# Twelve units instead of sixteen turned by TensorE, and part of VectorE's early work on GpSimd

## The chip, the cores and the metric

The kernel runs on one core of a Trainium2 chip. The metric is the device time of one execution in microseconds. PE is TensorE, DVE is VectorE, ACT is ScalarE, POOL is GpSimd and SP is SyncE, whose queue issues most of the loads.

## What is computed

A recurrent attention block (RWKV5) feeds a dense block with the activation h - tanh(h). Everything is float32, apart from the two weight matrices, which arrive as float64 and are converted on the chip.

```python
# r, k, v: (4, 8, 768, 48); w, u: (8, 48); w_in: (384, 2048); w_out: (2048, 384)
for t in range(S):
    kt, vt, rt = (k[:, :, t], v[:, :, t], r[:, :, t])
    cur = np.einsum('bhd,bhe->bhde', u[None] * kt, vt)
    y[:, :, t] = np.einsum('bhd,bhde->bhe', rt, state + cur)
    state = w[None, :, :, None] * state + np.einsum('bhd,bhe->bhde', kt, vt)
...
x = np.ascontiguousarray(attn_out.transpose(0, 2, 1, 3)).reshape(B * S, H * D)   # (3072, 384)
h = x @ w_in
g = h - np.tanh(h)
return (g @ w_out).astype(np.float32)
```

## The kernel before

**Attention in 24 units.** A unit (function `unit`, L754) is 64 time steps of two batches (one per half of the 128 partitions), all eight heads. `kw` is k times falling powers of the decay (L951). r and k must be turned so that the head dimension lies on the partitions. In the first way, used by units 0 to 15, PE turns r and kw with four transposes each (`turn`, L793 to L795) into the PSUM tile `x_ps`; DVE scales r by the table `w_up` (L799) and ACT copies k (L832). In the second way, used by units 16 to 23, r and k are loaded a second time: SP spreads them with eight small DMAs each into places inside `parts` (`spread_out`, L806 to L814), DVE turns 32x32 squares (L818) and multiplies by the powers of the decay or their reciprocals (L819). PSUM then holds only `yk_ps`.

After that a unit goes on alike: PE multiplies the state by rT (`from_state`) and kT by rT (`levels`), DVE copies the lower triangle of the levels into `at` (L981), PE multiplies `at` by v and kw by v (`outputs`, `to_state`; all of these matmuls carry the line L750), ACT copies the result to `xt` and `rest` (L910), and DVE adds to the state (L937) and lets it decay (L990). The diagonal of `at` is r times k (L836) times u (L971), summed (L840), written by ACT (L844). In the second way the state products come first and an ACT copy of two numbers (L872) stands between them and the levels. Unit n works on the state of unit n - 2.

**Dense part in 12 blocks of two units.** Block j has 256 tokens; its `xt` is completed by six POOL DMAs from `rest` (L931). A tile (function `hidden`, L1030) is two of the 16 slices of the inner dimension: PE computes h (L169), ACT five functions of it (L178 to L186), DVE four operations that end in g (L193 to L199), and PE multiplies g by w_out. There are two ways for that last product. The plain one is four products of 384 columns (L207). The other makes seven products of 192 columns (L258) from sums of g, which POOL makes (L243 to L247), and from sums of w_out, `mixed`, which DVE makes once (L267: four groups of four operations); it needs four PSUM banks that the first way of the units uses as `x_ps`.

**Passes.** For blocks 0 to 5, a first and a second pass over four slices each and a third over eight (`PASSES = 4, 4, 8`); sums between passes lie in `parts`. The third pass uses the seven products, so it starts after the last unit of the first way, after the weights' conversion (L137 to L143: five DVE and two ACT operations for each of 16 pieces) and after the mixing of its slices. Blocks 6 to 11 follow, each in one pass but the last. The places for the second way's loads lie in the part of `parts` that belongs to blocks 0 to 2, and come free in the third pass, when `gather` (L290) has read them.

**The order of all instructions** is found at build time by a planner (class `Plan`, L302). Each task has an engine, a cost, tasks that it follows, and a due time. `forward` simulates the engines, each taking the ready task that is due first; `backward` works out latest times; `search` changes due times at random and keeps what does not lengthen the simulated end. `order` (L479) first searches 2500 times up to 240 us (`BUSY`), then 500 times over the whole. Before the change all units are planned in the first way; then the registered changes turn units 16 to 23 to the second way (`change`, L326), and 500 more tries move only what starts after 240 us. The resulting list is emitted as it is, each engine in its order; waits come from the real data dependencies. `fills` (L683) puts idle matmuls into PE's gaps at the start.

Of the kernel before, what the change touches and what calls it, by code (L numbers as in the profile page):

```python
# [11 lines left out]
F32 = mybir.dt.float32  # L12
# [18 lines left out]
SHORT = 64  # L31
# [10 lines left out]
SEVEN = 8  # L42

# [102 lines left out]
class Dense:  # L146
# [114 lines left out]
    def mix(self, f, x):  # L261

        n, w, pairs = self.d.DM // 2, self.w_out_sb.rearrange("p (f z) n -> p f z n", z=2)[:, f], self.seven.mixed[:, f]
        b11, b12, b21, b22 = w[:, :, 0, :n], w[:, :, 0, n:], w[:, :, 1, :n], w[:, :, 1, n:]
        out, a, b, op = [(0, b11, b12, ALU.subtract), (1, b22, pairs[:, :, 0], ALU.add), (2, b22, b12, ALU.subtract),
                         (3, pairs[:, :, 1], b21, ALU.subtract)][x]
        self.nc.vector.tensor_tensor(pairs[:, :, out], a, b, op)  # L267
# [34 lines left out]
class Plan:  # L302
# [12 lines left out]
    def __init__(self):  # L315
        self.tasks, self.fills, self.changes = [], [], []

    def add(self, engine, cost, run, after=(), due=1e9, data=0, gated=False, steps=0):
        t = SimpleNamespace(engine=engine, cost=cost, run=run, after=[x for x in after if x], due=due, data=data,
                            gated=gated, steps=steps, then=[], n=len(self.tasks))  # L320
        for x in t.after:
            x.then.append(t)
        self.tasks.append(t)
        return t

    def change(self, t, **new):  # L326

        self.changes.append((t, new))
# [149 lines left out]

    def order(self, first=2500, tries=500):  # L479
# [18 lines left out]
        self.search(due, tries, chance, 0.0)  # L498

        for t, new in self.changes:  # L500
            for x in t.after:
                x.then.remove(t)
            vars(t).update(new)
            t.after = [x for x in t.after if x]
            for x in t.after:
                x.then.append(t)
        for _ in range(4):
            plan = self.forward(self.due)
            latest = self.backward(plan)
            self.due = [old if start < self.BUSY else new for old, new, start in zip(self.due, latest, plan[1])]  # L510
        plan = self.search(self.due, tries, chance, self.BUSY)
# [28 lines left out]
def near(ctx, tc, r, k, v, w, u, out, shared, moe_w_in, moe_w_out):  # L540
# [20 lines left out]
    plan = Plan()  # L561
    add = plan.add
# [6 lines left out]

    spread = parts.rearrange("q a n -> q (a n)")  # L570
    blocks = [spread[:, i * 512 : (i + 1) * 512].rearrange("q (x b e) -> q x b e", x=2 * NP, b=SHORT // 32) for i in range(4)]
    again = spread[:, 2048 : 2048 + NP * (SHORT + 1)].rearrange("d (p n) -> d p n", p=NP)
# [83 lines left out]
    inverse = work.tile([128, NP, SHORT + 1], F32, name="inverse", tag="tg")  # L656
    w_up = fixed("w_up", [128, NP, 2, SHORT])
# [25 lines left out]
    def fills(to):  # L683
        def run(n):
# [6 lines left out]
    now = [add(e, 1.25 if e == "ACT" else .87, lambda e=e, at=at, x=x: e_of[e].dma_start(out=rows[at : at + NP, :, :D], in_=x.rearrange("(p i) d -> p i d", i=2)), due=-1, data=.05)  # L691
           for e, at, x in (("SP", 0, w), ("ACT", NP, u))]
    cols = add("PE", .25, lambda: T.transpose(cols_ps, rows.rearrange("p i d -> p (i d)"), ident[: 2 * NP, : 2 * NP]), now)


    now = add("DVE", .45, lambda: V.tensor_scalar(
        by[:, :, 1:], wcol[:, :, None].to_broadcast([128, NP, SHORT]), W_LOW, W_HIGH, ALU.max, ALU.min), [cols])
    now = add("DVE", .7, lambda: V.tensor_tensor_scan(
        power.rearrange(flat), by.rearrange(flat), plus.rearrange(flat), 0.0, ALU.mult, ALU.add), [now])

    ups = add("ACT", .6, lambda: A.copy(w_up, power[:, :, None, :SHORT].to_broadcast([128, NP, 2, SHORT])), [now])
    now = add("DVE", 1.75, lambda: V.reciprocal(inverse, power), [now])
    inverted = now
    doubled = add("ACT", .6, lambda: A.copy(twice, inverse[:, :, None, 1:].to_broadcast([128, NP, 2, SHORT])), [now])
    now = tabled = add("PE", .7, table, [doubled], steps=8)
    downs = add("ACT", .5, lambda: A.copy(w_down, tab.rearrange("s (h d) -> s h d", h=H)[:, :, :D]), [now])
    keeps = add("ACT", .2, lambda: A.copy(saved, cols_ps), [cols])
    w_us = add("POOL", .2, lambda: G.tensor_tensor(w_u, saved[:, :NP], saved[:, NP:], ALU.mult), [keeps])
    now = add("POOL", 1.0, bounds, [keeps])
    now = add("PE", .2, lambda: T.matmul(tab[0:1, 0:1], ok[:, 0, :1], shared["one"], start=True, stop=True), [now, downs])  # L710
    flagged = add("DVE", .15, lambda: V.tensor_scalar(shared["flag"], tab[0:1, 0:1], 128 * NP - 0.5, None, ALU.is_lt), [now])
    bonus = add("SP", .65, lambda: Q.dma_start(
        out=ub.rearrange("p h d -> p (h d)"),
        in_=bass.AP(tensor=u.tensor, offset=u.offset, ap=[[0, 128], [1, H * D]])), data=.7)

    add("ACT", 1.3, lambda: A.activation(fixed("warm", [128, 1]), shared["one"], AF.Tanh), due=0)


    def steps(generator):

        made = []

        def step():
            if not made:
                made.append(generator())
            next(made[0])

        return step

    loads, converted = [], []  # L730
    for n in range(weights.count):

        queues, data = (("SP",), (3.0,)) if n % 4 > 1 else (("SP", "POOL") * 2, (1.2, .95) * 2)
        of = [add(e, .55, lambda n=n, i=i, e=e: weights.load(n, i, e_of[e]), [converted[n - 4] if n >= 4 else None],
                  data=x, gated=True) for i, (e, x) in enumerate(zip(queues, data))]
        if weights.sources[n % 4 > 1].dtype != I64:
            converted.append(of[-1])
            continue
        step = steps(lambda n=n: weights.convert(n))
        now = of + ([converted[n - 2]] if n >= 2 else [])  # L740
        for name, cost in (("DVE", .47), ("DVE", .47), ("ACT", .84), ("ACT", .84), ("DVE", .87), ("DVE", .87), ("DVE", .87)):
            now = [add(name, cost, step, now)]
        converted += now


    def flat4(t):
        return t.rearrange("d p z t -> d (p z t)")

    def put(*args, **how):
        T.matmul(*args, skip_group_check=True, **how)  # L750

    units, filled, last_h = [], {}, {}

    def unit(n):  # L754
# [3 lines left out]
        ch, half = divmod(n, 2)  # L758
        j, slot = divmod(n, L)
        steps_at = slice(ch * SHORT, (ch + 1) * SHORT)  # L760
        t = SimpleNamespace(at=ats[n % 2])
        rt, vt, kw, state = rts[n % (AHEAD + 1)], vts[n % (AHEAD + 1)], kws[n % 2], states[half]
        two = n >= L * (FIRST + 2)
        pair = yk_ps if two else x_banks[n == 1]
        sign = -1.0 if slot and j in dense.negative else 1.0
        r_ps, k_ps = (pair[:, i] for i in range(2))
        lev, own_lev = (pair[:, :, at : at + 256].rearrange("s i (p t) -> s i p t", p=NP) for at in ((256, 0) if two else (0, 256)))
        none = SimpleNamespace(**{x: None for x in "r k v turn rT kw kT rk du own diag state lev cp out xt rest add decay".split()})
        b1, b2, b3 = (units[n - i] if n >= i else none for i in (1, 2, 3))
        x = SimpleNamespace(rest=None, rk=None, du=None, own=None)  # L770
        units.append(x)
        product = n < OWN
        swap = n >= SWAP


        direct = j == 0

        def fetch(name, src, after):
            def run(z):
                if name == "k" and not hasattr(t, "kt"):  # L780
                    t.kt = first_k[slot] if direct else load.tile([128, H, D], F32, name="kt", tag="kt")
                to = {"r": rt, "v": vt}.get(name)
                Q.dma_start(out=(t.kt if to is None else to)[HALF[z], :, :D],  # L783
                            in_=src[half * 2 + z, :, steps_at, :].rearrange("h t d -> t h d"))

            of = [add("SP", .65, lambda z=z: run(z), after, data=.71) for z in range(2)]
            return add("none", 0, lambda: None, of)

        x.r = fetch("r", r, [b3.turn, b3.rk, b1.r])
        x.k = fetch("k", k, [b3.kw, b3.rk, b1.k])  # L790
        x.v = fetch("v", v, [b3.out, b1.v])

        def turn(src, to):  # L793
            for p in range(NP):
                T.transpose(to[:, p * C : (p + 1) * C], src[:, 2 * p : 2 * p + 2, :].rearrange("t h d -> t (h d)"), ident)  # L795
# [26 lines left out]
        def across_r():  # L822
            t.rT = across("rT", 0, power[:, :, :SHORT])
# [601 lines left out]
```

## Time and profile before

| | us |
|---|---|
| median of 3 runs (lowest, highest) | 591.65 (591.44, 592.0) |
| the profiled execution | 591.61 |
| its span | 589.5 |
| busy in it: PE, DVE, ACT, POOL | 571.2, 484.1, 398.9, 208.3 |
| last of the weights' conversion ends (L143) | 203.6 |
| mixing on DVE (L267), first start to last end | 208.4 to 236.4 |
| first of the seven products (L258) | 226.4 |
| first load of the second way (L813) | 268.3 |

The span runs from the first to the last instruction; the execution's time has some 2 us around it. Engines work side by side, so busy times don't add up to the span. A row of a group gives line, engine, operation, output and inputs with their shapes, count, then busy time and mean duration in ns, then the idle time ahead of it and what ended it. Durations of neighbours on PE and DVE overlap slightly; the distance between two starts is what one of them costs its engine.

### The profile page before, as it was taken

The numbers are of one execution on the slowest core, as the hardware profiler recorded it, in microseconds if no ns is written. First come the engines' busy times: TensorE is split into PE (matmuls) and PEld (weight loads), VectorE is DVE, ScalarE is ACT, GpSimd is POOL, SyncE is SP. The second block draws the span as 40 slices with busy tenths as digits, with TensorE's granted clock in tenths as the row PEclk, the third lists the DMA queues.
The fourth block names the chain that finished last, engine by engine and source line by source line (L and its number), as shares of the span: only waits on it lengthen the run. The fifth ranks groups of instructions, "written<-read, shape, count | busy, mean of one in ns | idle before, by whom it ended". The sixth has DMA issues, their size and how long they took to land.

```text
span 589.5 us, 14312 instructions
## 1 busy us (share of the span) xinstructions
PE 571.2 (97%) x5525; PEld 485.0 (82%) x5525; DVE 484.1 (82%) x806; ACT 398.9 (68%) x894; POOL 208.3 (35%) x366
## 2 busy tenths in 40 slices
PE   8888999999999989999999999999999999999996
PEld 5566677777777768999999998989999888999995
DVE  5699969999999999988779889697775896555666
ACT  3698888989686975775555566565665785476652
POOL 6002212201000143555554544483344554363420
PEclk9999999999999999999999999999999999999999
DMA  6976995954411310203111412244121220100101
GB/s 118 201 155 129 161 204 107 126 132 86 93 54 28 62 30 21 39 16 61 36 26 24 85 28 30 40 83 69 35 30 19 38 40 1 25 11 2 28 1 31
DMA packets 121141, 36.91 MB, mean 63 GB/s; under 512 B 113352, under 2 KB 115496, under 8 KB 121064
## 3 DMA queue, kind: packets, MB, share of 16 engines
q1 hardware_dynamic: 115900, 28.73, 26.9%
q0 software_dynamic: 4992, 6.99, 5.4%
q8 instruction: 45, 0.74, 0.5%
q14 instruction: 32, 0.26, 0.1%
q10 hardware_dynamic: 172, 0.20, 0.1%
HBM read 30.08 MB, written 4.72 MB: 59 GB/s over the span
## 4 chain that ended last, share of the span: by engine, by line
PE 76%; DVE 11%; ACT 4%; issue 3%; DMA 3%; SPq 2%; POOL 0%; DVEq 0%; ACTq 0%; POOLq 0%
PE h L169 37%; PE p L258 27%; PE o L207 5%; PE yk_ps L750 5%; SPq L783 2%; DMA st<-in_moe_w_in_dram 2%; DVE tg L197 1%; DVE g L193 1%; DVE tg L195 1%; DVE g L199 1%; DVE rT L799 1%; ACT at L844 1%; ACT s L178 1%; PE x_ps L795 1%; DMA kt<-in_k_dram 1%
## 5 line engine op out<-in xcount | busy, mean ns | idle before, releaser
L169 PE MATMUL h<-xt,w_in_sb 128*128 128x256 f32 x1152 | 281.0, 381 | 1.1 <-DVE w_in_sb L143 0.9
L169 PEld LDWEIGHTS h<-xt,w_in_sb 128*128 128x128 f32 x1152 | 212.9, 190 | 31.4 <-PE x_ps L795 1.1
L243 POOL TENSOR_TENSOR sg<-g 128x256 f32<-128x256 f32 x69 | 53.8, 780 | 144.6 <-DVE g L199 72.5
L258 PE MATMUL p<-mixed,sg 128*128 128x192 f32 x426 | 104.0, 326 | 0.0
L193 DVE TENSOR_TENSOR g<-h,th 128x512 f32<-128x512 f32 x96 | 65.8, 685 | 33.2 <-ACT s L178 14.3
L182 ACT ACTIVATE tg<-h 128x512 f32<-128x512 f32 x96 | 57.2, 596 | 48.3 <-PE h L169 48.2
L195 DVE SCALAR_TENSOR_TENSOR tg<-s,tg 128x512 f32<-128x512 f32 x96 | 68.3, 712 | 25.9 <-ACT tg L182 13.8
L180 ACT ACTIVATE th<-h 128x512 f32<-128x512 f32 x96 | 57.4, 598 | 43.0 <-PE h L169 42.8
L931 POOL DMA_DIRECT2D xt<-rest x66 | 32.3, 496 | 146.0 <-ACT rest L910 146.0
L178 ACT ACTIVATE s<-h 128x512 f32<-128x512 f32 x96 | 57.4, 598 | 39.1 <-PE h L169 38.8
L199 DVE COPY_PREDICATED g<-small,tg 128x512 f32<-128x512 int32 x96 | 76.0, 793 | 4.0
L258 PEld LDWEIGHTS p<-mixed,sg 128*128 128x128 f32 x426 | 75.1, 190 | 0.0
L197 DVE SCALAR_TENSOR_TENSOR tg<-q,tg 128x512 f32<-128x512 f32 x96 | 68.5, 715 | 7.5 <-ACT q L184 4.1
L207 PE MATMUL o<-w_out_sb,g 128*128 128x384 f32 x192 | 69.8, 490 | 1.7 <-DVE g L199 1.6
L258 PE MATMUL p<-w_out_sb,g 128*128 128x192 f32 x284 | 71.1, 332 | 0.0
L184 ACT ACTIVATE q<-s,m1b 128x512 f32<-128x512 f32 x96 | 69.5, 724 | 0.8
L186 ACT ACTIVATE small<-s,smallb 128x512 f32<-128x512 f32 x96 | 69.3, 722 | 0.5
L258 PEld LDWEIGHTS p<-w_out_sb,g 128*128 128x128 f32 x284 | 52.5, 190 | 7.4
L844 ACT ACTIVATE at<-same,du 128x64 f32<-128x64 f32 x184 | 47.7, 343 | 5.7 <-DVE du L840 5.6
L207 PEld LDWEIGHTS o<-w_out_sb,g 128*128 128x128 f32 x192 | 35.5, 190 | 18.4 <-issue 1.9
L245 POOL TENSOR_TENSOR sg<-sg,g 128x128 f32<-128x128 f32 x69 | 44.6, 647 | 5.1
L247 POOL TENSOR_TENSOR sg<-sg,g 128x128 f32<-128x128 f32 x69 | 39.0, 566 | 5.1
(131 smaller groups left out, 684.4 us busy)
## 6 DMA issues: line engine op xcount, KB each, us to landing
st<-in_moe_w_out_dram SPq DMA_DIRECT2D x8, 768.0 KB, 5.4
rt<-in_r_dram SPq DMA_DIRECT2D x48, 96.0 KB, 3.3
vt<-in_v_dram SPq DMA_DIRECT2D x48, 96.0 KB, 2.9
st<-in_moe_w_in_dram SPq DMA_DIRECT2D x16, 288.0 KB, 5.1
kt<-in_k_dram SPq DMA_DIRECT2D x44, 96.0 KB, 3.3
out_dram<-o POOLq DMA_DIRECT2D x44, 96.0 KB, 2.3
st<-in_moe_w_in_dram POOLq DMA_DIRECT2D x16, 96.0 KB, 5.1
xt<-rest POOLq DMA_DIRECT2D x66, 16.0 KB, 2.3
```

Source lines behind the costliest of these rows:

```text
L169: self.nc.tensor.matmul(t.h2[:, z], self.w_in_sb[:, t.f // 2, kk, z * 128 : (z + 1) * 128], self.xts[t.j][:, kk].rearrange("p b t -> p (b ...
L178: A.activation(out, t.h, AF.Square)
L180: A.activation(out, t.h, AF.Tanh)
L182: A.activation(out, t.h, AF.Tanh, scale=G1)
L184: A.activation(out, t.s, AF.Square, bias=self.m1b)
L186: A.activation(out, t.s, AF.Relu, bias=self.smallb, scale=-1.0)
L193: V.tensor_tensor(t.g, t.h, t.th, ALU.subtract)
L195: V.scalar_tensor_tensor(t.tg, t.s, C4, t.tg, ALU.mult, ALU.mult)
L197: V.scalar_tensor_tensor(t.tg, t.q, K1, t.tg, ALU.add, ALU.mult)
L199: V.copy_predicated(t.g, t.small.bitcast(I32), t.tg)
L207: self.nc.tensor.matmul(self.outs[i], t.g2[:, z, i * C : (i + 1) * C], self.w_out_sb[:, t.f + z, :], start=t.first and z == 0, stop=t.last ...
L258: self.nc.tensor.matmul(ps[bank][:, half * n : (half + 1) * n], a, b, start=t.first and half == 0, stop=t.last, skip_group_check=True)
```

## The change

1. Units 0 to 11 (before: 0 to 15) take the first way, 12 to 23 the second. The third pass now follows unit 11, and the second way's first loads follow the gathers of blocks 0 to 2.
2. The mixing of w_out (16 operations) moves from DVE to POOL.
3. For units 8 to 11, four operations each move from DVE to POOL: kw, r times k, that times u, and the decay of the state.
4. The planner builds two plans. A simpler one has sixteen units in the first way and all others turned by PE, as the plan of before had ahead of its registered changes. The real one takes the simpler one's due times for tasks that start there before 90 us (`ALIKE`), and finds the others by five rounds of `forward` and `backward` and 500 tries (`follow`). Registered changes are gone. The planner's cost for a second-way turn is 1.4 instead of 1.22.
5. `inverse` gets a place of its own, so the second reciprocal (L827) goes; the table `w_up` goes, and r is scaled by the powers themselves, read twice through a broadcast.

The body of `near` from the first task on becomes a function `lay_out(early, across_by)`. Without the change of indentation, the core of the diff is:

```diff
+ALIKE = 90.0
+EASED = 8
...
-        self.nc.vector.tensor_tensor(pairs[:, :, out], a, b, op)
+        self.nc.gpsimd.tensor_tensor(pairs[:, :, out], a, b, op)
...
+    def follow(self, other, until, tries=500):
+        theirs = {t.key: (other.due[t.n], t.start) for t in other.tasks}
+        kept = [theirs[t.key][0] if theirs.get(t.key, (0, until))[1] < until else None for t in self.tasks]
+        def pinned(due):
+            return [y if y is not None else x for x, y in zip(due, kept)]
...
+        for _ in range(5):
+            plan = self.forward(pinned(due))
+            due = self.backward(plan)
+        return self.listed(self.search(pinned(due), tries, Random(5), until))
...
-    inverse = work.tile([128, NP, SHORT + 1], F32, name="inverse", tag="tg")
-    w_up = fixed("w_up", [128, NP, 2, SHORT])
+    inverse = fixed("inverse", [128, NP, SHORT + 1])
...
-        two = n >= L * (FIRST + 2)
+        two = n >= early
+        turned = two and across_by == "DVE"
...
+        eased = across_by == "DVE" and EASED <= n < early
+        V_or_G, own_at = (G, ("POOL", 1.0)) if eased else (V, ("DVE", .47))
...
-            V.tensor_tensor(flat4(t.rT), r_ps, flat4(w_up), ALU.mult)
+            V.tensor_tensor(t.rT, r_ps.rearrange("d (p z t) -> d p z t", p=NP, z=2),
+                            power[:, :, None, :SHORT].to_broadcast([128, NP, 2, SHORT]), ALU.mult)
...
-            if n == L * (FIRST + 2):
-                V.reciprocal(again, power)
-            t.kT = across("kT", 1, again[:, :, 1:])
+            t.kT = across("kT", 1, inverse[:, :, 1:])
...
+        if turned:
+            freed = sum((gathered[y] for y in range(3)), []) if n < early + 2 else []
+            in_r = add("SP", 4.8, lambda: spread_out(r, 0), [b2.rT, *freed], data=.8)
+            in_k = add("SP", 4.8, lambda: spread_out(k, 1), [b2.kT, *freed], data=.8)
+        x.turn = None if turned else add("PE", .46, lambda: turn(rt, r_ps), [x.r] + free, steps=8)
+        x.kw = add(*own_at, lambda: V_or_G.tensor_tensor(kw[:, :, :D], t.kt[:, :, :D], w_down, ALU.mult), [x.k, downs, b2.out])
+        x.turn_k = x.rk = None if turned else add("PE", .46, lambda: turn(t.kt if direct else kw, k_ps), [x.k if direct else x.kw] + free, steps=8)
...
+        x.rT = add("DVE", 1.4, across_r, [in_r, b1.lev]) if turned else add("DVE", .62, scale_r, both + [ups])
+        if turned:
+            x.kT = add("DVE", 1.4, across_k, [in_k, b1.lev])
...
+            x.rk = add(*own_at, own, [x.r, x.k, b2.du, b1.rk if not b1.own else None])
+            now = add(*own_at, lambda: V_or_G.tensor_tensor(t.rk, t.rk, ub, ALU.mult), [x.rk, bonus])
...
+        x.decay = x.add if not ch else add(*own_at, lambda: V_or_G.tensor_tensor(state[:, :, :, :D], state[:, :, :, :D], w_all, ALU.mult), [x.add]) if more else None
...
+                now = add(*(("POOL", 1.05) if across_by == "DVE" else ("DVE", .47)), run, converted + [now])
...
-            done = units[L * (FIRST + 2) - 1]
+            done = units[early - 1]
...
-    for t in plan.order():
+    simpler = lay_out(L * (FIRST + 2), "PE")
+    simpler.order()
+    plan = lay_out(L * FIRST, "DVE")
+    for t in plan.follow(simpler, ALIKE):
```

## The prediction

> **What bounds the kernel now.** I read the page's busy rows first, then stretches of the span, because a mean over a start, a middle and a tail says little.
>
> ```profile
> span 589.5 us, 14312 instructions
> PE 571.2 (97%) x5525; PEld 485.0 (82%) x5525; DVE 484.1 (82%) x806; ACT 398.9 (68%) x894; POOL 208.3 (35%) x366
> ...
> 0.00:90.00 90.00, 79.28 (x1452) 56.16 (x1453) 73.00 (x135) 66.48 (x193) 20.38 (x59) 1.00 0.86 161
> 90.00:225.00 135.00, 132.08 (x1255) 99.50 (x1255) 132.10 (x215) 109.48 (x230) 19.26 (x35) 1.00 0.38 77
> 225.00:285.00 60.00, 59.96 (x378) 55.55 (x378) 52.35 (x90) 39.84 (x85) 31.23 (x48) 1.00 0.20 36
> 285.00:510.00 225.00, 224.99 (x2023) 205.35 (x2022) 177.74 (x286) 138.13 (x306) 109.77 (x174) 1.00 0.21 38
> ```
>
> The columns are the stretch, its length, then busy time of PE, PEld, DVE, ACT and POOL, the clock and the DMA share. From 90 us on PE is the bound: it idles 2.9 of 135 us in the second stretch and nothing in the next two. DVE is as full as PE from 90 to 225 (132.1 of 135), and has 47 us free from 285 to 510. POOL is nearly unused before 225. So time is won in two ways: fewer PE instructions, or an end to those 2.9 us. PE's waits in 120 to 225 name who ends them, both DVE operations of units 14 and 15:
>
> ```profile
> PE x_ps L795 <- DVE at L981: 1.4, 1, 1.4
> PE yk_ps L750 <- DVE state L937: 0.6, 1, 0.6
> ```
>
> **PE's part of the change.** Four units (12 to 15) lose two groups of four transposes each. I price a group by the distance between starts in PE's order of time, not by its busy time, since matmuls overlap.
>
> ```profile
> 200.60 0.60 PE L795 MATMUL x_ps<-ident,kw 128*128 128x128 f32 x4
> 201.03 1.46 PE L169 MATMUL h<-xt,w_in_sb 128*128 128x256 f32 x6
> ...
> 205.35 1.46 PE L169 MATMUL h<-xt,w_in_sb 128*128 128x256 f32 x6
> 206.74 0.69 PE L750 MATMUL yk_ps<-rT,state 48*64 48x64 f32 x32
> 207.26 0.65 PE L750 MATMUL x_ps<-rT,kT 48*64 48x64 f32 x32
> 207.84 1.56 PE L169 MATMUL h<-xt,w_in_sb 128*128 128x256 f32 x6
> ...
> 353.82 0.49 PE L258 MATMUL p<-w_out_sb,sg 128*128 128x192 f32 x2
> 354.24 0.69 PE L750 MATMUL yk_ps<-rT,kT 48*64 48x64 f32 x32
> 354.86 0.59 PE L258 MATMUL p<-w_out_sb,g 128*128 128x192 f32 x2
> ```
>
> A group takes 201.03 - 200.60 = 0.43 us (0.49 elsewhere), so two take 0.9. But the second way splits state products from level products (an ACT copy stands between). Joined, as at 206.74, they take 1.10 plus 0.10 at each edge (half an h takes 1.29 undisturbed, 1.39 here): 1.30. Split, the second piece, at 354.24, takes 0.62 plus 0.10 on each side, 0.82, and the first, at 348.55 in the same view, 0.83: 1.65. Net per unit 0.9 - 0.35 = 0.55; four units give **2.2 us**. All of it is on the path, as PE is the path.
>
> **The stretch 90 to 225.** DVE loses there the work of units 12 to 15. By the groups' means a unit is kw 0.588, rk 0.576, times ub 0.597, du 0.543, rT 0.684, cp 0.726, state 0.547 and decay 0.561: 4.8 us, four are 19. Sixteen operations of units 8 to 11 (four of each of kw, rk, times ub, decay) go to POOL: 4 x 2.32 = 9.3. The sixteen of mixing cost DVE 5.9 + 2.7 + 2.2 = 10.8. That is 39 us less, against 132 used (part of the 9.3 lies before 90 us). With DVE at some three quarters, the 2.9 us should mostly go. Bounds: all stay (0) or all go (2.9). I take **1.9**, the two waits above plus rounding down, as both belong to units that leave.
>
> **POOL's new work.** No row shows a 128x384 tensor-tensor on POOL. The nearest rows are its sums of g; uncontended ones take 0.46 us at 128 elements and 0.73 at 256, slowest ones 0.97 and 1.17. A line through the fast pair gives 0.99 at 384, an estimate; below it stands 0.73 (the smaller shape), above it 1.4 (1.17 plus one such step). 32 x 0.99 = 32 us (23 to 45), in a stretch with POOL busy 19 of 135. It is cover enough, provided the queue behind (POOL's loads of w_in, fills of xt) is not late: a fill waits behind at most one chain of a unit, some 3 us, and xt is filled well ahead.
>
> What POOL costs DVE is seen on DVE's own rows: the masked copy without POOL beside it, and with it.
>
> ```profile
> L199 DVE COPY_PREDICATED g<-small,tg 128x512 f32<-128x512 int32 x19 | 13.9, 730 | 0.1
> ...
> L199 DVE COPY_PREDICATED g<-small,tg 128x512 f32<-128x512 int32 x22 | 19.5, 889 | 1.3
> ...
> L243 POOL TENSOR_TENSOR sg<-g 128x256 f32<-128x256 f32 x21 | 16.9, 806 | 35.0 <-PE p L258 34.9
> ```
>
> The first row is 90 to 205 us, the others 225 to 330. L197's mean goes from 683 to 734 ns, L195's from 682 to 692. Over 61 POOL sums of 42 us together DVE lost 22 x 0.16 + 21 x 0.05 + 21 x 0.01 = 4.8 us, 0.11 per POOL us. So 32 us cost DVE 3.7, out of 39 saved.
>
> The Trainium skill speaks against the move: "SBUF — State Buffer", section "Who interferes with whom", says that a DVE instruction with two SBUF inputs and a GpSimd instruction that reads SBUF lock each other out for their whole length. Were DVE the loser every time, the 39 us saved would be nearly given back, and the 1.9 with it (589.4). The row shows that POOL is often the one that waits: its 128x128 sum takes 0.46 or about 0.8.
>
> **After 225.** The third pass needs unit 11 instead of unit 15, so it starts earlier by what units 12 to 15 took of PE: 4 x (1.3 + 1.2 for outputs + 0.9) = 13.6. It begins at about 226.4 - 13.6 = 213. These four come back as turned units: transposes 0.699 + 0.692 and products 0.744 + 0.730, 2.87, instead of rT's 0.684: 7.0 us a unit, **28 us** into DVE's free 47. Per block of 39 + 5.7 = 44.7 PE us (8 tiles of 4.87, two units of 2.85), DVE needs 8 x 2.9 + 14.0 + 2.3 = 39.5: 88%. Its pieces at 315 to 330 and 465 to 480, at 14.55 and 14.79 of 15, left PE at 15.00, so I cost this at nothing; without that cover the excess goes onto the path. Those 39.5 are overlapping busy times, which leaves more room, not less. On ACT the kT copy (0.586) gives way to a 0.137 one.
>
> SP issues 16 more small loads a unit, 4 to 5 us per eight, landing in 2.1. Unit 16's k now goes out at 268.3, right after the third pass's block 1 gave its output to POOL (267.2): the loads wait for the place in parts that they overwrite, not for the planner's date. Earlier loads are hidden.
>
> At nothing too: no w_up (0.62 on ACT, beside the reciprocal of 1.78), no second reciprocal (1.76 on DVE, beside a full PE), rT's product from a broadcast operand (a broadcast one, L803, takes 0.686; L799 0.684), inverse in its own place. Up to 90 us due times are those of before, so I leave the 10.7 us of PE idle there; POOL's decay, 0.43 slower than DVE's, may add up to 4 x 0.43 = 1.7 to waits for state at 88 and 96 us, or DVE's relief may take away the 1.3 that they are now.
>
> **Sum.** The profiled run took 591.61 us (2.1 outside its span), 0.04 from the median 591.65. 591.6 - 2.2 - 1.9 = **587.5**, 0.7% less.
>
> **Rivals.**
> - Stalls stay or move: planner and chip differ by as much as before. 591.6 - 2.2 = 589.4, up to 590.4 with 1 us of new waits. For: the search after 90 us is only 500 tries. Against: slack on DVE.
> - Mixing comes late. Now the last conversion ends at 203.6 and mixing at 236; the third pass takes it from 213. If conversions keep their date, POOL's eight operations of the groups needed first end at 203.6 + 8 = 211.6, after which sums of g (2 us) follow on the same queue: just in time. All sixteen first: 203.6 + 16 + 2 = 221.6, 8.6 late, 596.1. Against: DVE's 39 us let conversions finish earlier. The middle, 3 to 5 us late, is 590.5 to 592.5: no change.
> - Slower: **units 12 and 13 are late for block 6.** Their places are free by plan only when block 2 of the third pass is gathered: 213 + 3 x 19.5 + 3 = 274. Block 6 begins at 213 + 117 = 330, its first h some 10 us (two tiles) sooner, 320. A fast unit runs 8 us from state products to outputs (469.95 to 477.76), so loads 12, two units 20 and the fill 5 are done at 311. At the present pace of 20 to 25 us a unit it is 274 + 12 + 45 + 5 = 336, up to 16 late, with half of it covered by tiles in hand: 8, so 595.5. It decides from 4.1 us late on. For: DVE is dense there. Against: nothing else claims DVE's free 45%, and the loads can go out earlier.
> - Better: waits at 75 to 105 go too, or conversions shift: 585 to 586.5.
>
> **Chances.** Forecast 587 to 589 0.45, stalls stay 0.17, better 0.12, mixing around no change 0.09, late units or mixing by more 0.17. Some 0.2% (1.2 us) is what a measurement can tell from no change. So faster 0.74, same 0.09, slower 0.17. The range leaves out the best and the worst tenth: 584.5 to 594.5.
>
> **What would show it.** L795 x_ps groups fall from 128 matmuls to 96 and L818 rises from 16 to 24 transposes; PE busy falls by about 2; PE idle from 90 to 213 is under 1.5; L267 stands on POOL at 0.8 to 1.3 us; DVE is at about 90% from 275 to 500 with PE full. PE idle near 211 to 222 with POOL mixed as releaser would show the second rival, idle near 320 to 335 with xt or rest behind it the third. Idle before 90 us that differs by over 1.5 would make the forecast wrong in a place that I costed at nothing.

## The result, and the profile after

The changed kernel takes 599.77 us (median of 4 runs, 597.68 to 600.49) against 591.55 before (4 runs): ratio of the means 1.0132, interval 1.0106 to 1.0159. It is slower by 1.3%; 0.7% faster was forecast, and the range ended at 594.5. The profiled run took 600.49 us, and by its own span and stretches (page, then the same stretches as before; columns: stretch, length, busy PE, PEld, DVE, ACT, POOL, clock, DMA share, GB/s):

```profile
span 598.8 us, 14367 instructions
...
PE 572.9 (96%) x5493; PEld 484.4 (81%) x5493; DVE 487.4 (81%) x785; ACT 395.6 (66%) x893; POOL 240.4 (40%) x398
```

```profile
0.00:90.00 90.00, 78.56 (x1387) 55.11 (x1387) 70.62 (x123) 63.41 (x181) 30.00 (x68) 1.00 0.82 160
90.00:225.00 135.00, 125.94 (x852) 94.77 (x853) 128.05 (x186) 98.69 (x197) 44.03 (x52) 0.97 0.34 70
225.00:285.00 60.00, 60.00 (x322) 56.15 (x322) 42.56 (x73) 35.12 (x65) 29.36 (x50) 1.00 0.19 34
285.00:510.00 225.00, 224.39 (x2351) 202.03 (x2350) 189.64 (x308) 150.15 (x360) 106.08 (x176) 1.00 0.29 49
```

Nearly the whole loss lies ahead of 225 us. PE idles 9.1 us between 90 and 225, where it idled 2.9, and in that stretch alone the granted clock is 0.97. DVE, which was to have a quarter of its time free there, is busy 128 of 135 us with 29 instructions fewer (186, not 215). What PE waited for, from 60 to 120 us and from 120 to 225 (in each row the us in total, the times, and the longest):

```profile
PE yk_ps L760 <- DVE at L993: 2.3, 2, 1.3
PE yk_ps L760 <- DVE rT L814: 2.0, 1, 2.0
PE yk_ps L760 <- DVE state L951: 1.8, 2, 1.0
...
```

```profile
PE p L260 <- DVE parts L222: 2.8, 1, 2.8
PE o L209 <- DVE parts L222: 1.6, 1, 1.6
...
```

The first three are the chains of the units, from 60 us on. In the last two, PE can't overwrite a PSUM bank until DVE has added it to `parts`: DVE is late with everything. Why, DVE's rows from 190 to 222 us show, beside POOL's mixing there (L201 was L199 before, L199 was L197, L195 was L193, L222 was L220):

```profile
L201 DVE COPY_PREDICATED g<-small,tg 128x512 f32<-128x512 int32 x6 | 6.0, 1000 | 0.2
L199 DVE SCALAR_TENSOR_TENSOR tg<-q,tg 128x512 f32<-128x512 f32 x5 | 5.4, 1081 | 0.1
...
L195 DVE TENSOR_TENSOR g<-h,th 128x512 f32<-128x512 f32 x5 | 3.4, 679 | 0.0
...
L222 DVE TENSOR_TENSOR parts<-o,parts 128x384 f32<-128x384 f32 x4 | 2.2, 542 | 0.0
```

```profile
L269 POOL TENSOR_TENSOR mixed<-w_out_sb 128x384 f32<-128x384 f32 x8 | 9.5, 1207 | 51.6 <-DVE w_out_sb L145 51.6
```

The masked copy (L201) and L199 read two operands from SBUF; they take 1.00 and 1.08 us on average, where they took 0.73 and 0.68 from 90 to 205 us before the change. L195 and L222 read one of theirs from PSUM; they keep 0.68 and 0.54. POOL's mixing takes 1.2 to 1.4 us an operation on average. One by one, a DVE operation with two SBUF inputs takes about twice its time or more beside a mixing operation. The first row below starts while POOL mixes, the second in a pause of mixing:

```profile
193.31 1.35 DVE L983 TENSOR_TENSOR rk<-rk,ub 128x384 f32<-128x384 f32 x1
...
206.06 0.55 DVE L983 TENSOR_TENSOR rk<-rk,ub 128x384 f32<-128x384 f32 x1
```

The account of the span, 9.3 us longer: PE idle +7.6 (+4.9 from 60 to 120, +2.5 from 195 to 230, the rest small) and PE busy +1.7, although 32 matmuls went. Without the clock PE's busy time would have fallen by some 1.3: after the 2.8 us wait PE worked some 6.1 us at half the clock, which cost it 3.0 (below).

### The profile page after: what moved, and what is told of

It reads as the page before. It is cut to its first block, busy times and chain, and to the rows that moved or that the text cites. A ratio compares the mean times of both kernels' runs of the same rounds, so it can differ in the third digit from the quotient of the medians.

```text
span 598.8 us, 14367 instructions
## 1 busy us (share of the span) xinstructions
PE 572.9 (96%) x5493; PEld 484.4 (81%) x5493; DVE 487.4 (81%) x785; ACT 395.6 (66%) x893; POOL 240.4 (40%) x398
## 4 chain that ended last, share of the span: by engine, by line
PE 78%; DVE 11%; SPq 4%; issue 2%; DMA 2%; ACT 1%; POOL 0%; DVEq 0%; ACTq 0%; POOLq 0%
PE h L171 37%; PE p L260 28%; PE o L209 7%; PE yk_ps L760 5%; SPq L798 3%; SPq L125 1%; DMA kt<-in_k_dram 1%; DVE tg L197 1%; DVE tg L199 1%; DVE rk L850 1%; DMA st<-in_moe_w_out_dram 1%; DVE power L144 1%; DVE g L195 1%; DVE du L854 1%; DVE rT L814 1%
## 5 line engine op out<-in xcount | busy, mean ns | idle before, releaser
L197 DVE SCALAR_TENSOR_TENSOR tg<-s,tg 128x512 f32<-128x512 f32 x96 | 74.0, 771 | 43.4 <-ACT tg L184 30.8
L195 DVE TENSOR_TENSOR g<-h,th 128x512 f32<-128x512 f32 x96 | 65.6, 684 | 28.1 <-ACT s L180 13.9
L201 DVE COPY_PREDICATED g<-small,tg 128x512 f32<-128x512 int32 x96 | 73.4, 766 | 4.2 <-DVE tg L199 0.5
L199 DVE SCALAR_TENSOR_TENSOR tg<-q,tg 128x512 f32<-128x512 f32 x96 | 69.9, 728 | 4.2 <-ACT q L186 0.8
L247 POOL TENSOR_TENSOR sg<-sg,g 128x128 f32<-128x128 f32 x69 | 40.4, 587 | 4.8
L249 POOL TENSOR_TENSOR sg<-sg,g 128x128 f32<-128x128 f32 x69 | 38.4, 557 | 4.8
```

The source lines that it names most:

```text
L195: V.tensor_tensor(t.g, t.h, t.th, ALU.subtract)
L197: V.scalar_tensor_tensor(t.tg, t.s, C4, t.tg, ALU.mult, ALU.mult)
L199: V.scalar_tensor_tensor(t.tg, t.q, K1, t.tg, ALU.add, ALU.mult)
L201: V.copy_predicated(t.g, t.small.bitcast(I32), t.tg)
```

## The experiments

Theory A at the start: POOL's operations and DVE's with two SBUF inputs hold each other up, so that the moved work relieves nobody. Rival B: the new planning is at fault. Rival C: the four units cost time in the late part. The later rivals stand with their runs. Line numbers are those of the changed kernel.

**mix_back**: mixing on DVE again, in the planner too.

```diff
-        self.nc.gpsimd.tensor_tensor(pairs[:, :, out], a, b, op)
+        self.nc.vector.tensor_tensor(pairs[:, :, out], a, b, op)
...
-                    now = add(*(("POOL", 1.05) if across_by == "DVE" else ("DVE", .47)), run, converted + [now])
+                    now = add("DVE", .47, run, converted + [now])
```

> Mixing goes back to VectorE, in the planner too; the rest is the changed kernel (600.5 us in its profiled run). Theory A, that GpSimd's 16 mixing operations and VectorE's operations with two SBUF inputs hold each other up: VectorE's operations of 1.0 us between 190 and 222 us return to 0.7, the wait ahead of the first of the seven products falls from 2.8 us to under 1, the clock keeps 1.00 there, and the time falls by 4 to 6 us, to 594 to 596. Rival B, that the new planning is at fault: the order of the work stays poor and the time stays at 598 to 601.

595.82 us (4 runs), ratio to before 1.0077 (1.0060 to 1.0095). The wait ahead of the first products is 0.8, the clock there 1.00, and the three operations with two SBUF inputs (L197, L199, L201) take 0.70 to 0.77. As A said. (The clock of its profiled run fell at 94 us instead, and cost PE 1.6 us.)

**own_back**: `EASED = 12`, so units 8 to 11 keep their operations on DVE; mixing stays on POOL.

> The sixteen operations of units 8 to 11 go back to VectorE, in the planner too; mixing stays on GpSimd. Theory A: TensorE's idle time from 75 to 120 us falls from some 6 us to 2 to 3, the stall at the first seven products stays, and the time falls by 3 to 4 us, to 596 to 597. Rival B: no change beyond 1 us, 599 to 601.

597.47 us (4 runs), ratio 1.0102 (1.0084 to 1.0120). PE idle from 60 to 120 falls to 2.3 (before: 2.1; changed kernel: 6.9). Only 2.3 us of the time come back, as the waits for `parts` grow to 5.7 in this order of the work.

**both_back**: both edits.

> Both parts go back to VectorE; what is left is twelve units in the first way, the others turned by VectorE, and the new planning. Theory A: the gain of 2.2 us for the transposes comes out, with waits like those of the kernel before: 588 to 590. Rival B (the new planning): 595 or more. Rival C, that the four units that go to the late part cost time there: 592 to 595, with TensorE idle after 285 us.

590.65 us (10 runs), ratio 0.9987 (0.9977 to 0.9996): below the kernel before, though by 0.1%, and a little above A's range: of the 2.2 us that A expected back, 0.7 came. From 285 to 510 us PE is busy 224.6 of 225. B and C fall. The two parts on POOL cost 9.1 us together (599.77 to 590.65), more than 4.0 and 2.3 one by one (the end of this section returns to that).

**full_search**: `for t in plan.order():` in place of `plan.follow(simpler, ALIKE)`.

> The changed kernel, but the real plan is found by the full search with 2500 and 500 tries, with no due times taken from a simpler plan. Theory A: the operations on GpSimd remain, so the time stays within 2 us of the changed kernel, 598 to 602. Rival B: it falls below 594.

606.66 us (4 runs), ratio 1.0270 (1.0236 to 1.0303). Slower by 7 than the changed kernel. A's number was missed, B's more so. Whether the simpler plan's due times help, or this search only met a worse plan, one plan of each doesn't tell.

**Does the engine matter, or the plan?** Next the plan was held still.

**keep_mix**: only the `nc.gpsimd` of mixing becomes `nc.vector`; the planner still believes in POOL, so every engine keeps its order, with mixing put into DVE's.

> The plan of the changed kernel is kept, order and all; only the 16 mixing operations run on VectorE, at the places that the plan gave them on GpSimd. VectorE gets some 8 us more work of its own between 190 and 222 us and is no longer held up there. Theory A (the two engines hold each other up): VectorE's operations with two SBUF inputs go back to 0.7 us, and the time is 595 to 598, no worse than the changed kernel's 600 although VectorE does more. Rival B, that re-planning was what helped when mixing went back: 600 to 604.

600.73 us (4 runs), ratio 1.0156 (1.0137 to 1.0175). A's number was missed, and the time lies in B's range. DVE's operations are back at 0.7, as A said, and yet nothing is won over 599.77:

```profile
L201 DVE COPY_PREDICATED g<-small,tg 128x512 f32<-128x512 int32 x6 | 4.4, 725 | 0.1
L197 DVE SCALAR_TENSOR_TENSOR tg<-s,tg 128x512 f32<-128x512 f32 x6 | 4.3, 724 | 0.0
...
L199 DVE SCALAR_TENSOR_TENSOR tg<-q,tg 128x512 f32<-128x512 f32 x5 | 3.4, 678 | 0.0
```

Sixteen mixing operations on DVE cost it some 8 to 9 us, starts 0.46 to 0.54 apart. In the changed kernel DVE lost the same by being held up, from the rows of 190 to 222 us: L201 6 x 0.27, L199 5 x 0.40, L197 5 x 0.31 (1.00, not 0.69), and 3.0 on the products for r and k, 8.2 together. So theory A is amended: mixing on POOL costs DVE about what it costs on DVE. What mix_back won (4.0 us) came with its new plan, made with mixing as DVE's work.

**keep_mix_reads** and **keep_mix_sets**: as keep_mix, and beside each mixing operation POOL does something of no use, into a place in `last` that is free until the end. In the first it reads:

```diff
+        self.nc.vector.tensor_tensor(pairs[:, :, out], a, b, op)
+        self.nc.gpsimd.tensor_tensor(self.last.rearrange("p l (a n) -> p l a n", a=2)[:, 0], b11, b12, ALU.subtract)
```

and in the second it only writes: `for part in (self.last, self.last[:, 0]): self.nc.gpsimd.memset(part, 0.0)`.

> As keep_mix, and beside each of the mixing operations on VectorE GpSimd makes one subtraction of the same size from w_out into a place that nobody reads and nothing waits for. Theory A: nothing waits for these results, and still VectorE's operations with two SBUF inputs take 1.0 us or more beside them, and the time rises by 4 to 8 us over keep_mix, with TensorE waiting for sums in parts. Rival D, that the harm came from waiting for mixing on GpSimd's queue: no more than 1 us over keep_mix, apart from the queue's delay of the sums of g.

> As keep_mix_reads, but GpSimd only writes there (two memsets, some 1.2 us together) instead of reading. If it is the reading that holds VectorE up, its operations stay at 0.7 us and the time is within 1.5 us of keep_mix; if any GpSimd operation does it, or the queue, the time is that of keep_mix_reads.

607.78 us (4 runs), ratio 1.0275 (1.0257 to 1.0293), and 601.12 us (4 runs), ratio 1.0169 (1.0144 to 1.0194). Reads that nobody waits for cost 7.0 us over keep_mix, writes 0.4, which is within the scatter of the runs. Not all of the 7.0 is waiting: in the profiled runs, which lie 7.4 apart, PE lost 6.5 us to a halved clock with the reads and 1.6 in keep_mix, and 1.7 of the 6.5 fell at 25 to 30 us, ahead of all mixing. DVE's and POOL's rows from 190 to 222 us, of keep_mix_reads:

```profile
L269 DVE TENSOR_TENSOR mixed<-w_out_sb 128x384 f32<-128x384 f32 x6 | 5.3, 888 | 0.0
L197 DVE SCALAR_TENSOR_TENSOR tg<-s,tg 128x512 f32<-128x512 f32 x5 | 4.8, 959 | 0.0
...
L195 DVE TENSOR_TENSOR g<-h,th 128x512 f32<-128x512 f32 x4 | 2.7, 680 | 0.0
...
L270 POOL TENSOR_TENSOR last<-w_out_sb 128x384 f32<-128x384 f32 x10 | 12.5, 1246 | 32.1 <-DVE w_out_sb L145 31.5
```

and of keep_mix_sets:

```profile
L269 DVE TENSOR_TENSOR mixed<-w_out_sb 128x384 f32<-128x384 f32 x8 | 4.9, 609 | 0.0
...
L195 DVE TENSOR_TENSOR g<-h,th 128x512 f32<-128x512 f32 x6 | 4.1, 682 | 2.0 <-ACT s L180 2.0
L197 DVE SCALAR_TENSOR_TENSOR tg<-s,tg 128x512 f32<-128x512 f32 x5 | 3.7, 731 | 0.0
...
L271 POOL MEMSET last<- 128x768 f32 (+1 forms) x15 | 8.8, 587 | 0.7
```

L269 and L197, with two SBUF inputs, grow from 0.61 and 0.73 to 0.89 and 0.96 beside reads; L195, with one, stays at 0.68. The masked copy (L201) keeps 0.72 in both; with the reads, none of its five starts while POOL reads. It is POOL's reading that holds DVE up. Rival D (waiting for mixing in POOL's queue) falls, since nothing waits for these reads.

**clock_fill**: the changed kernel, with three idle matmuls ahead of the first of the seven products, into the PSUM tile that is free then.

```diff
         if dense.seven.ps is None:
+            for _ in range(3):
+                fills(yk_ps[:, 0])[0][1]()
             banks_now[1].close()
```

> The changed kernel with three idle matmuls of 128x512 (some 2.4 us together) on TensorE ahead of the first of the seven products, where it waited 2.8 us and the granted clock then stood at 0.50 to 0.71 for 7 us. Theory E, that the wait makes the clock fall: the clock keeps 1.00 from 210 to 225 us and the time falls by 2.5 to 3.5 us, to 596.5 to 597.5, though no wait is shorter. Rival F, that the clock falls for another cause: it still falls there, and the time stays at 599 to 601.

598.06 us (4 runs), ratio 1.0104 (1.0087 to 1.0121). The two stretches at the wait, first of the changed kernel, then of clock_fill (the number after POOL's is the clock):

```profile
210.00:215.00 5.00, 2.23 (x8) 1.80 (x7) 4.97 (x8) 2.79 (x5) 4.33 (x4) 0.73 0.09 16
215.00:220.00 5.00, 5.00 (x18) 4.44 (x17) 4.48 (x5) 0.00 (x0) 4.84 (x6) 0.58 0.21 39
```

```profile
210.00:215.00 5.00, 4.74 (x17) 2.59 (x16) 5.00 (x7) 2.79 (x5) 4.33 (x5) 1.00 0.17 33
215.00:220.00 5.00, 5.00 (x29) 4.69 (x28) 4.86 (x6) 0.83 (x2) 4.84 (x6) 1.00 0.24 43
```

Theory E holds: with the wait filled the clock keeps 1.00 there, and PE gets 29 matmuls done in 215 to 220 us instead of 18. In the changed kernel the halved clock takes 5 x (0.27 + 0.42) = 3.4 us of these two stretches, 0.4 of it in the wait itself and 3.0 of PE's work. The gain between the medians is 1.7 us, less than expected, and the profile shows where 1.7 went: in clock_fill's run the clock fell after an earlier wait, one of 2.0 us that ended at 101 us. The changed kernel has the same wait (L814 above) and kept its clock there. First the changed kernel, then clock_fill:

```profile
100.00:105.00 5.00, 3.89 (x135) 3.30 (x136) 4.40 (x8) 4.04 (x13) 3.83 (x7) 1.00 0.57 128
105.00:110.00 5.00, 4.75 (x82) 3.60 (x82) 4.74 (x8) 4.90 (x15) 1.02 (x1) 1.00 1.18 171
```

```profile
100.00:105.00 5.00, 4.13 (x86) 3.15 (x90) 4.39 (x8) 4.24 (x14) 3.63 (x7) 0.74 0.50 119
105.00:110.00 5.00, 5.00 (x90) 3.98 (x86) 3.96 (x7) 4.24 (x12) 0.72 (x1) 0.92 1.16 180
```

The changed kernel's own runs point the same way: the fastest of the four (597.68 us) has a mean clock of 0.999 over its span, the others (599.43 to 600.49) 0.992 to 0.994.

**keep_own**: the plan is kept, `V_or_G = V`, with the planner still told `("POOL", 1.0)`.

> The changed kernel's plan is kept; only the sixteen operations of units 8 to 11 run on VectorE, at the places that the plan gave them on GpSimd; mixing stays on GpSimd. Theory A1, that their length on GpSimd (1.0 to 1.7 us each where VectorE takes 0.55) delays the chain of these units: TensorE's idle time from 60 to 120 us falls from 6.9 us to 3 to 5, and the time to 597 to 598.5. Theory A2, that they, too, give VectorE no net relief and only re-planning helps: idle time of 6 to 8 us, 599 to 601.

600.24 us (4 runs), ratio 1.0153 (1.0137 to 1.0168). PE idles 5.4 us from 60 to 120, between the ranges of A1 and A2, and the time is A2's. DVE is held up in the changed kernel here too, and no longer in keep_own, as L197 shows from 70 to 108 us (changed kernel, then keep_own):

```profile
L197 DVE SCALAR_TENSOR_TENSOR tg<-s,tg 128x512 f32<-128x512 f32 x3 | 3.2, 1079 | 1.5 <-ACT s L180 1.5
```

```profile
L197 DVE SCALAR_TENSOR_TENSOR tg<-s,tg 128x512 f32<-128x512 f32 x3 | 2.1, 684 | 1.5 <-ACT s L180 1.5
```

Yet the other engine alone gives no time: 1.5 us of idle time went from 60 to 120, and the profiled runs are 0.5 us apart.

**real_costs**: `("POOL", 1.25)` and `("POOL", 1.35)` in the planner.

> The changed kernel, with the planner told what the trace shows for GpSimd: 1.25 instead of 1.0 for the operations of units 8 to 11, 1.35 instead of 1.05 for mixing. It still doesn't know that VectorE is held up. Theory A: that is the larger part, so 596 to 600. Rival G, that GpSimd's own length was the mis-sized cost: 591 to 594.

602.26 us (4 runs), ratio 1.0178 (1.0162 to 1.0194). Rival G falls, and A's range was missed by 2: the better number for POOL alone made the plan no better.

**late_groups**: as both_back, with mixing of the two groups that only blocks 6 to 11 need on POOL: `(self.nc.gpsimd if f.start < 4 else self.nc.vector)`, and the same in the planner.

> As both_back, but the two groups of mixing that only blocks 6 to 11 need (8 operations) stay on GpSimd, where they can run after 225 us. Theory A: VectorE has room there, so nothing is lost, and up to 1 us may be won around 205 to 245 us, where VectorE was full: 589.5 to 591. If any mixing on GpSimd costs as much: 592 to 594.

594.80 us (5 runs), ratio 1.0055 (1.0041 to 1.0069). The planner, which sees no harm in POOL, put these eight operations at 187.5 to 199.7 us, not after 225, and PE waited 3.4 us for `parts`. The time is above both ranges. So this is once more the price of mixing on POOL beside a full DVE: 4.1 us over both_back, of which some 3.0 are the clock, halved for 6.8 us after that wait; whether it would be free after 225 was not tried.

**more_tries**: both_back with `tries=1500` in `follow`.

> As both_back, with 1500 instead of 500 tries in the last search. If what is left of waits (some 6 us from 60 to 285 us) is the search's, 588.5 to 590; if the chip differs from the planner's model, no change: 590 to 591.5.

589.06 us (5 runs), ratio 0.9962 (0.9948 to 0.9976): the fastest of all, 0.4% under the kernel before. PE's wait for `parts` is then:

```profile
PE p L260 <- DVE parts L222: 0.4, 1, 0.4
...
```

It differs from both_back in the number of tries alone, and the two lie 1.6 us apart. No kernel was planned with other random tries of the same number, so a difference of that size between two plans may be the search's.

The falls of the clock also account for what POOL's two parts seemed to cost more together than one by one. They took 3.0 us of PE's work in the profiled run of the changed kernel, 1.6 in mix_back, 3.9 in own_back and nothing in both_back. If these are subtracted from the times of the profiled runs (an estimate), mixing's return to DVE wins 3.7 us, that of the units' operations 4.3, and both together 6.8: no more than the sum.

## Why the prediction was wrong

**The step that failed** is "what POOL costs DVE": 0.11 us of DVE per us of POOL, 3.7 us in all. That was a mean over 225 to 330 us, where DVE has gaps (busy 90.6 of 105 us) and POOL's operations are short sums. From 190 to 219 us DVE has hardly a gap. There 8.2 us were lost beside 18.7 us of mixing: 0.44 per us, four times as much (0.33 if the 6.3 us of POOL's sums in that window are counted too). So the "39 us less" for DVE did not come, and the 1.9 us of waits to be won turned into 6.1 us more of them. Of the 12.3 us between 587.5 and 599.8, 9.1 go when POOL's two parts go (both_back). The Trainium skill's rule that the prediction weighed ("SBUF — State Buffer", "Who interferes with whom": a DVE instruction with two SBUF inputs contends with a GpSimd instruction that reads SBUF, not with one that only writes) is what the runs show, in the three cases tried, L197 and L195 as examples: 0.73 us grow to 0.96 beside reads and stay at 0.73 beside memsets, and the 0.68 with one input from PSUM stay throughout. The prediction preferred a mean from another stretch to it.

A second step failed beside it: "DVE at some three quarters" does not follow from less work. In both_back nothing new runs on POOL and units 12 to 15 are gone from the stretch, and still DVE is busy 130.2 of 135 us:

```profile
90.00:225.00 135.00, 132.36 (x848) 101.27 (x847) 130.23 (x209) 102.85 (x201) 20.90 (x35) 1.00 0.32 68
```

Its freed time went into work that was brought forward: the conversion ends at 188.9 us instead of 203.6, and the first of the seven products starts at 204.1 instead of 226.4.

- **PE's part**, 2.2 us: its size is near. By distances between starts, summed over the span, transposes fall from 15.4 to 11.8 us in both_back, and state products and levels rise from 26.5 to 27.2: 2.9 net. Yet both_back gains 0.7 and more_tries 2.2; in both_back the products of the dense part's tiles take 487.3 us by the same measure, not 484.8. Why was not tested.
- **POOL's operations**: 0.99 was the value, 0.73 to 1.4 the bounds. Mixing took 1.21 to 1.30 by group, the operations of units 8 to 11 1.05 to 1.21. Inside the bounds, but above the value.
- **Up to 90 us nothing**, at most 1.7: right. PE idles 11.4 us there instead of 10.7. But the chains of units 8 to 11 go on behind 90 us, where nothing was allowed for them: of the 4.9 us by which PE idle rose from 60 to 120, 3.5 lie from 90 to 120. own_back takes 4.6 of the 4.9 back.
- **After 225**: right. DVE is busy 189.6 of 225 us from 285 to 510, PE 224.4. Units 12 and 13 were not late; the rival that was to make it slower did not happen.
- **The rival of late mixing** had the place (211 to 222 us, first of the seven products), but gave it 8.6 us, where PE lost some 5.5 (2.5 more idle from 195 to 230, 3.0 of clock), and the wrong mechanism: PE waited for sums in `parts` from a DVE held up by mixing, not for mixed weights.
- **Missing altogether**: the clock that falls after a wait, 3.0 us of PE's work here.
- What would show it: L810's groups are 96 and L834's 24, as said; PE busy rose by 1.7 instead of falling by 2, because of the clock: less its 3.0 us it fell by 1.3.

What stays open: why real_costs is slower than the changed kernel, and how much of mix_back's and own_back's gain is the planner's knowing better and how much is one plan happening to be better than another.

## What to carry to other kernels

Work that was moved to GpSimd, and reads SBUF there, did not relieve a VectorE without gaps whose operations read two operands from SBUF. Price such a move from a stretch as full as the one it goes to. A planner that doesn't know of the contention can pack work into time that isn't there: hold its order still and change only the engine to tell the two apart. Where TensorE must wait for 2 us or more, look at the clock behind the wait; idle matmuls in it kept the clock here.

## What the runs showed of the hardware

- A halved clock came in steps: in the profiles of these runs each fall of the granted clock to 0.50 that ended within the span lasted 3.4 or 6.8 us. In the changed kernel it was 6.8, from 212 to 219 us, after a wait of 2.8 us between matmuls.
- The length of a wait did not decide alone. The wait of 2.0 us at 101 us was followed by a fall in clock_fill and by none in the changed kernel and in keep_mix; one of 3.4 us at 130 in full_search was followed by none. The Trainium skill ("TensorE: Matmul & The Clock Gate", "Part 1") gives half the clock after an idle window of about 3.4 us: the half agrees; here waits of 2.0 and 2.8 us could suffice.
- POOL's writing alone (16 pairs of memsets) cost 0.4 us in the whole kernel, within the scatter; 16 reads in the same places of the order cost 7.0, a part of it by the clock.
- Two SBUF inputs were not the only DVE form that POOL's reads held up. In the changed kernel one operation of the conversion with a single input from SBUF (L140, 0.55 us before and in the other rows) took 1.36 us beside kw on POOL, and ended only after it. The reduction L854, the product L195 and the sum into `parts` (L222), with one SBUF input each, kept their times beside POOL's mixing.

```profile
86.45 1.36 DVE L140 TENSOR_SCALAR w_in_sb<-st 128x768 uint32<-128x768 uint32 x1
```

```profile
86.20 1.19 POOL L966 TENSOR_TENSOR kw<-kt,w_down 128x384 f32<-128x384 f32 x1 [1.72 <-PE yk_ps L760]
```
